# Gradient loads moved to the ScalarE queue and copies of P moved to GpSimd, in a fused window-attention forward and backward kernel

## Chip, cores, metric

One core of one Trainium2 chip. The metric is the device time of one execution in microseconds. All times are medians over the runs of one kernel. Runs are marked fast or slow (slow: over 1.5% above the fastest run of the same kernel). A ratio is the mean time of one kernel's fast runs over the mean of the other's fast runs of the same rounds, so it is not quite the ratio of the medians quoted beside it. Engines: PE is TensorE (matmuls), PEld its weight loads, DVE is VectorE, ACT is ScalarE, POOL is GpSimd, SP is SyncE. A "q" behind the name (SPq, ACTq) means the engine's sequencer, which issues DMAs. A DMA has landed when the semaphore (a counter that engines wait on) that tells of its end is full; its landing time is counted from its issue.

## The reference

Attention in windows of 8x8 tokens on a 256x256 picture with 384 channels, and its gradients. There is one head, and each window attends within itself.

```python
def _fwd_reference(x, wqkv, wo):            # x (1,256,256,384), cut to what matters
    xw = ...                                # 1024 windows of 64 tokens
    q, k, v = split(xw @ wqkv)
    p = softmax(q @ k.T * C ** -0.5)        # 64x64 per window
    return ((p @ v) @ wo).reshape(...)

def reference(x, wqkv, wo, grad_out):
    out, vjp = jax.vjp(_f, x, wqkv, wo)
    return (out, *vjp(grad_out))            # out, dx, dwqkv, dwo, all bfloat16
```

## The kernel before

The kernel works on 128 "quads" of four tiles, a tile being two windows (128 tokens on the 128 partitions). It is software-pipelined: in step i it takes quad i+1 through the projections (`A`), quad i through scores, softmax (whose first instruction on DVE takes the row maximum, `mx`) and half of its attention (`B`), quad i-1 through the other half (`C`), and quad i-2 through dx (`D`). The tile `xq` holds x, `dq` the incoming gradient. Four transposes a quad are done by DMA, all issued from SyncE: `dT` and `xT` (dq and xq with channels on the partitions), `tok` (`yz`, the output of the projections, turned to tokens) and `UT` (`Uq`, that is dS times x, turned for dx).

```python
def load(st):
    ...
    for t in range(QUAD):
        nc.sync.dma_start(out=xq[:, t, :], in_=dram_tile(x, bp, t0 + t))
        nc.gpsimd.dma_start(out=dq[:, t, :], in_=dram_tile(grad_out, bp, t0 + t))

# soft(), step 3, part 1: P into its places of the block tile ps
    for w, h in ((0, LO), (1, HI)):
        nc.scalar.copy(out=ps[h, :, w, :], in_=st["Pb"][h, :, :])

def step(d, c, b, a):          # "[...]" marks cuts
    B(scores) [... softmax of b on DVE/ACT between PE's values and projections ...]
    filler(1)                                   # PE: 12 matmuls of a weight gradient
    pw = C_(attend, (2, 3))                     # ACT copies osb, DVE copies Uq
    C_(to_channels, "Uq", "UT")                 # DMA transpose from SyncE
    C_(attend_end, (2, 3), pw)                  # ACT and DVE copy Wq
    D_(dx_tokens, (0, 1))
    turn_end(b, turn(b))                        # PE: pt; DVE: PS
    D_(dx, (0, 1))                              # PE: UT @ AT_sb; ACT copies dsb
    filler(1)
    pw = B(attend, (0, 1)) [...]
    D_(dx_tokens, (2, 3)); D_(dx, (2, 3))

for i in range(-1, n + 2):                      # LEAD = 3
    d, c, b, a = get(i - 2), get(i - 1), get(i), get(i + 1)
    to_channels(get(i + 2), "dq", "dT")         # SyncE: dT, xT, four xq, tok, then UT
    to_channels(get(i + 2), "xq", "xT")
    load(get(i + LEAD))
    to_tokens(c)
    step(d, c, b, a)
    [...]
```

All PSUM tiles come from one ring of eight. From `attend(2,3)` to `dx_tokens(0,1)` eight tiles are taken, so the next one, `pt` of `turn`, can only start when the first `osb` copy on ACT has freed its tile.

Of the kernel before, what the change touches and what calls it, by code (L numbers as in the profile page):

```python
# [17 lines left out]
QUAD = 4  # L18
# [4 lines left out]
def kernel(  # L23
# [12 lines left out]
    nc = tc.nc  # L36
# [7 lines left out]
    LEAD = 3  # L44
# [56 lines left out]
    def dram_tile(ap, bp, t):  # L101
        return ap[0, 2 * WIN * bp:2 * WIN * (bp + 1), WIN * t:WIN * (t + 1), :]
# [3 lines left out]
    def load(st):  # L106
        bp, t0 = st["at"]
        st["xq"] = xq = grp.tile([P, QUAD, C], BF16, tag="xq", name="xq", bufs=2 * GQ + 4)
        st["dq"] = dq = qp.tile([P, QUAD, C], BF16, tag="dq", name="dq", bufs=6)
        for t in range(QUAD):  # L110
            nc.sync.dma_start(out=xq[:, t, :], in_=dram_tile(x, bp, t0 + t))
            nc.gpsimd.dma_start(out=dq[:, t, :], in_=dram_tile(grad_out, bp, t0 + t))  # L112

    def to_channels(st, src, name):
        st[name] = dst = qp.tile([P, QUAD, CK, P], BF16, tag=name, name=name, bufs=3 if name == "xT" else 2)
        nc.sync.dma_start_transpose(out=dst[:].rearrange("p t m k -> p (t m) k"),
                                    in_=st[src][:].rearrange("p t c -> p (t c)"))
# [18 lines left out]
    def to_tokens(st):  # L136
        st["tok"] = tok = qp.tile([P, CK, QUAD, 2, P], BF16, tag="tok", name="tok")
        nc.sync.dma_start_transpose(out=tok[:].rearrange("p m t b k -> p (m t b) k"),
                                    in_=st["yz"][:].rearrange("p m t s k -> p (m t s k)"))
# [12 lines left out]
    def over_k(ap, n=P):  # L152
        return ap.unsqueeze(2).broadcast_to([n, QUAD, WT])

    def soft(st, step, part=0):
        sd = st["sd"]
        if step == 0:
            st["mx"] = mx = sm.tile([P, QUAD], F32, tag="mx", name="mx")
            for w, h in ((0, HI), (1, LO)):
                nc.vector.tensor_reduce(out=mx[h, :], in_=sd[h, :, w, :], axis=AX.X, op=ALU.max)  # L160
        elif step == 1:
            mx = st["mx"]
            st["sh"] = sh = sm.tile([P, QUAD, WT], F32, tag="sh", name="sh")
            for w, h, o in ((0, HI, LO), (1, LO, HI)):
                nc.vector.tensor_tensor(out=sh[o, :, :], in0=sd[h, :, w, :], in1=over_k(mx[h, :], WT),
                                        op=ALU.subtract)
        elif step == 2:
            st["ex"] = ex = sm.tile([P, QUAD, WT], F32, tag="ex", name="ex")
            nc.scalar.activation(out=ex[:], in_=st["sh"][:], func=ACT.Exp)  # L169
        elif step == 3 and part == 0:  # L170
            ex = st["ex"]
            rs = sm.tile([P, QUAD], F32, tag="rs", name="rs")
            nc.vector.tensor_reduce(out=rs[:], in_=ex[:], axis=AX.X, op=ALU.add)  # L173
            ri = sm.tile([P, QUAD], F32, tag="ri", name="ri")
            nc.vector.reciprocal(out=ri[:], in_=rs[:])
            st["Pb"] = Pb = qp.tile([P, QUAD, WT], BF16, tag="Pb", name="Pb")
            nc.vector.tensor_tensor(out=Pb[:], in0=ex[:], in1=over_k(ri[:]), op=ALU.mult)  # L177
        elif step == 3:
            st["ps"] = ps = qp.tile([P, QUAD, 2, WT], BF16, tag="ps", name="ps", bufs=3)
            for w, h in ((0, LO), (1, HI)):  # L180
                nc.scalar.copy(out=ps[h, :, w, :], in_=st["Pb"][h, :, :])
        elif step == 4:
            st["pr"] = pr = sm.tile([P, QUAD, WT], F32, tag="pr", name="pr")
            for w, h in ((0, LO), (1, HI)):
                nc.vector.tensor_tensor(out=pr[h, :, :], in0=sd[h, :, w, :], in1=st["Pb"][h, :, :], op=ALU.mult)  # L185
            st["D"] = D = sm.tile([P, QUAD], F32, tag="D", name="D")
            nc.vector.tensor_reduce(out=D[:], in_=pr[:], axis=AX.X, op=ALU.add)
        else:
            pd = sm.tile([P, QUAD, WT], F32, tag="pd", name="pd")
            nc.vector.tensor_tensor(out=pd[:], in0=st["Pb"][:], in1=over_k(st["D"][:]), op=ALU.mult)  # L190
            ps = st["ps"]
            for w, h, o in ((0, LO, HI), (1, HI, LO)):
                nc.vector.tensor_tensor(out=ps[o, :, w, :], in0=st["pr"][h, :, :], in1=pd[h, :, :], op=ALU.subtract)

    def turn(st):
        pt = ring.tile([P, QUAD, 2, WT], F32, tag="r", name="pt")
        for t in range(QUAD):
            both = st["ps"][:, t, :, :].rearrange("p w k -> p (w k)")
            for h in (LO, HI) if t < 2 else (slice(0, P),):
                nc.tensor.matmul(pt[h, t, :, :].rearrange("p s k -> p (s k)"), lhsT=both[:, h], rhs=ident[:],  # L200
                                 start=True, stop=True)
        return pt

    def turn_end(st, pt):
        st["PS"] = dst = qp.tile([P, QUAD, 2, WT], BF16, tag="PS", name="PS")
        nc.vector.tensor_copy(out=dst[:], in_=pt[:])
# [68 lines left out]
    def gf_group(sts):  # L275
        n = len(sts) * QUAD
        for f, rn in enumerate(("Uq", "Wq")):
            for ma in range(CK):
                pw = ring.tile([P, C], F32, tag="r", name="pg")
                for i in range(n):  # L280
                    st, t = sts[i // QUAD], i % QUAD
                    product(pw[:], st["xq"][:, t, ma * P:(ma + 1) * P], st[rn][:, t, :], i == 0, i == n - 1)
                nc.vector.tensor_tensor(out=GF_acc[:, f, ma, :], in0=pw[:], in1=GF_acc[:, f, ma, :], op=ALU.add)  # L283
                yield

    def filler(n):
        while n and fill:
            try:
                next(fill[0])
                n -= 1  # L290
            except StopIteration:
                fill.pop(0)

    def step(d, c, b, a):
        def on(st):
            return (lambda f, *r: f(st, *r)) if st is not None else (lambda f, *r: None)
        D_, C_, B, A = on(d), on(c), on(b), on(a)
        B(scores)
        B(soft, 0)
        B(soft, 1)  # L300
        B(values, 0)
        B(values, 1)
        B(values, 2)
        B(soft, 2)
        B(values, 3)
        B(soft, 3, 0)
        A(project, 0, 0)
        A(project, 0, 1)
        B(soft, 3, 1)
        A(project, 0, 2)  # L310
        B(soft, 4)
        A(project, 1, 0)
        B(soft, 5)
        A(project, 1, 1)
        A(project, 1, 2)
        filler(1)
        pw = C_(attend, (2, 3))
        C_(to_channels, "Uq", "UT")
        C_(attend_end, (2, 3), pw)
        D_(dx_tokens, (0, 1))  # L320
        if b is not None:
            turn_end(b, turn(b))
        D_(dx, (0, 1))
        filler(1)
        pw = B(attend, (0, 1))
        B(attend_end, (0, 1), pw)
        D_(dx_tokens, (2, 3))
        D_(dx, (2, 3))

    quads = [(bp, t0) for bp in range(NBP) for t0 in range(0, NT, QUAD)]  # L330
    sts = [{"at": q} for q in quads]
    n = len(sts)
    get = lambda i: sts[i] if 0 <= i < n else None
    with tc.manual_schedule(engines=MANUAL):
        for i in range(min(LEAD - 1, n)):
            load(sts[i])
        to_channels(sts[0], "dq", "dT")
        to_channels(sts[0], "xq", "xT")
        held = []
        for i in range(-1, n + 2):  # L340
            d, c, b, a = get(i - 2), get(i - 1), get(i), get(i + 1)
            if i + 2 > 0 and get(i + 2) is not None:
                to_channels(get(i + 2), "dq", "dT")
                to_channels(get(i + 2), "xq", "xT")
            if get(i + LEAD) is not None:
                load(get(i + LEAD))
            if c is not None:
                to_tokens(c)
            step(d, c, b, a)
            if c is not None:  # L350
                held.append(c)
            if held and (len(held) == GQ or i == n):
                fill.append(gf_group(held))
                held = []
            if 0 <= i - 2:
                sts[i - 2] = None
        filler(1 << 30)
# [62 lines left out]
```

## Time and profile before

| | before |
|---|---|
| time, median of 3 | 2122.46 us |
| a quad (span / 128, with the ends) | about 16.6 us |
| PE busy, idle | 1979 us, 142 us |
| SyncE's issues a quad, idle between them | 15.5 us, 0.8 us |

The page of the kernel before. The first line has the busy time of each engine, the next two what the packets of a DMA queue took as a share of 16 DMA engines' time (q1 is SyncE's queue, q0 GpSimd's), the last two the chain of work that ended last, by engine and by line.

```profile
PE 1979.2 (93%) x16510; PEld 1075.3 (51%) x16510; DVE 1268.9 (60%) x2851; ACT 1474.6 (70%) x3213; POOL 1124.8 (53%) x2054
...
q1 hardware_dynamic: 1074384, 304.15, 84.4%
q0 software_dynamic: 98304, 151.39, 26.9%
...
PE 55%; DMA 29%; DVE 7%; ACT 7%; issue 1%; POOL 0%; SPq 0%; ACTq 0%; POOLq 0%
DMA UT<-Uq 26%; PE pg L120 16%; PE pd L120 14%; PE pj L120 7%; PE pv L120 6%; ACT uq L219 5%; PE sd L147 4%; PE pd L262 4%; PE pu L237 3%; DMA tok<-yz 3%; DVE pr L185 2%; DVE rs L173 2%; ACT ex L169 2%; DVE Pb L177 2%; PE pw L237 1%
```

The two queues' packets add up to over 100%, because packets of different queues overlap on an engine. So the DMA engines are close to full. The timeline of SyncE (start, duration, what was issued) shows the queue that feeds them:

```profile
981.44 2.60 SPq L116 DMA_TRANSPOSE UT<-Uq  x1
984.26 3.20 SPq L116 DMA_TRANSPOSE dT<-dq  x1
987.64 2.82 SPq L116 DMA_TRANSPOSE xT<-xq  x1
990.52 2.54 SPq L111 DMA_DIRECT2D xq<-in_x_dram  x4
993.16 4.53 SPq L138 DMA_TRANSPOSE tok<-yz  x1
997.79 3.20 SPq L116 DMA_TRANSPOSE UT<-Uq  x1
```

There is no gap worth the name: 997.79 - 981.44 is one quad, and SyncE issues all through it. Since it runs late, PE waits for what it delivers. From the waits of the kernel before (who waited for whom: us in total, times, longest):

```profile
ACT osb L244 <- issue: 231.1, 152, 1.8
...
PE pd L262 <- DMA tok<-yz: 66.4, 57, 3.6
...
PE pd L120 <- DMA UT<-Uq: 53.0, 82, 2.9
```

ACT idles before `osb` copies with nothing to wait for (the first line), and PE's idle time is mostly for `UT` and `tok`. A piece of the timeline with ACT and PE at the first of these places; the bracket is idle time before, with what ended it:

```profile
1005.04 0.86 ACT L244 CAST osb<-po 128x384 bf16<-128x384 f32 x2 [1.50 <-issue]
...
1005.21 0.52 PE L262 MATMUL pd<-tok,ps 128*64 128x384 bf16 x4
1005.57 0.52 PE L200 MATMUL pt<-ident,ps 128*64 128x128 bf16 x6
```

`pt` follows at once, because `osb` was copied in time.

### The profile page before, as it was taken

The page shows a single profiled execution, that of the slowest core. Times are in us where ns is not written, and L with a number is a line of the kernel's source. Part 1 is how long each engine was busy: PE and PEld are TensorE (multiplying, and loading weights), DVE is VectorE, ACT ScalarE, POOL GpSimd, SP SyncE. Part 2 cuts the span into 40 slices and gives each one's busy share as a digit, 9 for nine tenths or more (in the row PEclk, how much of TensorE's full clock was granted, in tenths as well). Part 3 has the DMA queues.
Part 4 walks back from the last instruction along what each step waited for, and adds up shares of the span by engine and source line. Part 5 has one row for each costly group of instructions (what it writes and reads, how often), then busy time and mean ns, then how long its engine had stood idle before and what let it go on. Part 6 is the DMA issues. An engine that isn't in the chain of part 4 may idle for free.

```text
span 2121.0 us, 46307 instructions
## 1 busy us (share of the span) xinstructions
PE 1979.2 (93%) x16510; PEld 1075.3 (51%) x16510; DVE 1268.9 (60%) x2851; ACT 1474.6 (70%) x3213; POOL 1124.8 (53%) x2054
## 2 busy tenths in 40 slices
PE   7899999999999999989999998999999999999998
PEld 4455555555555555544555454555555454455554
DVE  6566566656656655655556555665566655556664
ACT  6677677767767767766667666776677766767773
POOL 4555555555555555555555455555555555555543
PEclk9999999999999999999999999999999999999999
DMA  9999999999999999999999999999999999999995
GB/s 208 219 221 224 214 224 229 225 217 211 224 230 217 226 218 219 219 217 206 219 217 216 205 226 213 212 215 216 228 217 220 221 216 216 212 219 225 225 222 124
DMA packets 1173319, 458.79 MB, mean 216 GB/s; under 512 B 1056864, under 2 KB 1147744, under 8 KB 1173088
## 3 DMA queue, kind: packets, MB, share of 16 engines
q1 hardware_dynamic: 1074384, 304.15, 84.4%
q0 software_dynamic: 98304, 151.39, 26.9%
q8 instruction: 129, 2.11, 0.5%
q14 instruction: 102, 0.84, 0.1%
q10 hardware_dynamic: 400, 0.29, 0.0%
HBM read 101.84 MB, written 101.84 MB: 96 GB/s over the span
## 4 chain that ended last, share of the span: by engine, by line
PE 55%; DMA 29%; DVE 7%; ACT 7%; issue 1%; POOL 0%; SPq 0%; ACTq 0%; POOLq 0%
DMA UT<-Uq 26%; PE pg L120 16%; PE pd L120 14%; PE pj L120 7%; PE pv L120 6%; ACT uq L219 5%; PE sd L147 4%; PE pd L262 4%; PE pu L237 3%; DMA tok<-yz 3%; DVE pr L185 2%; DVE rs L173 2%; ACT ex L169 2%; DVE Pb L177 2%; PE pw L237 1%
## 5 line engine op out<-in xcount | busy, mean ns | idle before, releaser
L226 POOL DMA_DIRECT2D out_dram<-osb x1024 | 580.5, 574 | 671.1 <-ACT osb L244 641.3
L244 ACT CAST osb<-po 128x384 bf16<-128x384 f32 x512 | 220.7, 483 | 411.7 <-issue 231.1
L283 DVE TENSOR_TENSOR GF_acc<-pg,GF_acc 128x384 f32<-128x384 f32 x258 | 143.9, 558 | 548.0 <-PE pg L120 548.0
L120 PEld LDWEIGHTS <-xq 128*128 128x128 bf16 x3072 | 304.9, 99 | 221.0 <-issue 14.3
L112 POOL DMA_DIRECT2D dq<-in_grad_out_dram x512 | 270.4, 534 | 190.2 <-DMA out_dram<-osb 172.2
L120 PE MATMUL pd<-AT_sb,UT 128*128 128x384 bf16 x1536 | 305.5, 337 | 53.5 <-DMA UT<-Uq 53.0
L228 POOL DMA_DIRECT2D out_dram<-dsb x512 | 275.9, 543 | 115.3 <-ACT dsb L270 101.3
L270 ACT CAST dsb<-pd 128x384 bf16<-128x384 f32 x512 | 229.6, 481 | 148.1 <-issue 111.6
L120 PE MATMUL pg<-Wq,xq 128*128 128x384 bf16 x1536 | 277.4, 332 | 0.0
L120 PE MATMUL pg<-Uq,xq 128*128 128x384 bf16 x1536 | 273.5, 329 | 0.0
L120 PE MATMUL pv<-B_sb,xT 128*128 128x384 bf16 x1536 | 271.4, 327 | 0.0
L120 PE MATMUL pj<-xT,A_sb 128*128 128x512 bf16 x1152 | 269.5, 379 | 0.7 <-DMA xT<-xq 0.7
L120 PE MATMUL pj<-dT,BT_sb 128*128 128x512 bf16 x1152 | 269.5, 379 | 0.0
L219 ACT CAST uq<-pv 128x384 bf16<-128x384 f32 x512 | 242.9, 475 | 36.3 <-PE pv L120 34.2
L245 DVE CAST Uq<-pu 128x384 bf16<-128x384 f32 x512 | 259.3, 548 | 3.1 <-PE pu L237 3.1
L256 ACT CAST Wq<-pw 64x384 bf16<-64x384 f32 x512 | 242.9, 474 | 9.2
L132 ACT CAST yz<-pj 128x512 bf16<-128x512 f32 x384 | 225.4, 587 | 4.3 <-PE pj L120 0.2
L120 PEld LDWEIGHTS <-UT 128*128 128x128 bf16 x1536 | 133.2, 99 | 171.1 <-DMA UT<-Uq 69.9
L134 ACT CAST yz<-pj 128x512 bf16<-128x512 f32 x384 | 201.3, 603 | 1.1 <-PE pj L120 1.0
L262 PE MATMUL pd<-tok,ps 128*64 128x384 bf16 x1024 | 133.4, 340 | 71.1 <-DMA tok<-yz 66.4
L120 PEld LDWEIGHTS <-xT 128*128 128x128 bf16 x1536 | 141.8, 98 | 83.4 <-issue 0.8
L120 PEld LDWEIGHTS <-A_sb 128*128 128x128 bf16 x1152 | 112.7, 98 | 136.9 <-DMA xT<-xq 1.2
(61 smaller groups left out, 2020.8 us busy)
## 6 DMA issues: line engine op xcount, KB each, us to landing
xq<-in_x_dram SPq DMA_DIRECT2D x512, 96.0 KB, 3.9
dq<-in_grad_out_dram POOLq DMA_DIRECT2D x512, 96.0 KB, 5.8
out_dram<-osb POOLq DMA_DIRECT2D x1024, 48.0 KB, 4.3
out_dram<-dsb POOLq DMA_DIRECT2D x512, 96.0 KB, 4.8
dT<-dq SPq DMA_TRANSPOSE x128, 5.5
xT<-xq SPq DMA_TRANSPOSE x128, 5.3
tok<-yz SPq DMA_TRANSPOSE x128, 10.0
UT<-Uq SPq DMA_TRANSPOSE x128, 6.1
```

What stands on the lines that cost most here:

```text
L112: nc.gpsimd.dma_start(out=dq[:, t, :], in_=dram_tile(grad_out, bp, t0 + t))
L120: nc.tensor.matmul(out, lhsT=lhsT, rhs=rhs, start=start, stop=stop)
L132: nc.scalar.copy(out=yz[:, mo, :, 0:4:3, :], in_=pj[:])
L134: nc.scalar.copy(out=yz[:, mo, :, 1:3, :], in_=pj[:])
L219: nc.scalar.copy(out=st["uq"][:, t, :], in_=pj[:])
L226: nc.gpsimd.dma_start(out=to[WIN * w:WIN * (w + 1)], in_=src[h, :])
L228: nc.gpsimd.dma_start(out=to, in_=src[:])
L244: nc.scalar.copy(out=osb[:], in_=po[:])
L245: nc.vector.tensor_copy(out=st["Uq"][:, t, :], in_=pu[:])
L256: nc.scalar.copy(out=st["Wq"][h, pair[1], :], in_=pw[1][o, :])
L262: nc.tensor.matmul(pd[o, :], lhsT=st["ps"][:, t, w, :], rhs=st["tok"][:, :, t, w, :], start=True, stop=False)
L270: nc.scalar.copy(out=dsb[:], in_=pd[:])
```

## The change

Its intent: GpSimd's queue carries all stores and the gradient loads; take the gradient loads off it, to a hardware-driven queue, and issue them from ACT exactly where ACT idles. ACT gets room for that by giving the two small copies of P to GpSimd.

```diff
-            nc.gpsimd.dma_start(out=dq[:, t, :], in_=dram_tile(grad_out, bp, t0 + t))
+    def load_grad(st, tiles):
+        bp, t0 = st["at"]
+        for t in tiles:
+            nc.scalar.dma_start(out=st["dq"][:, t, :], in_=dram_tile(grad_out, bp, t0 + t))
 [...]
-                nc.scalar.copy(out=ps[h, :, w, :], in_=st["Pb"][h, :, :])
+                nc.gpsimd.tensor_copy(out=ps[h, :, w, :], in_=st["Pb"][h, :, :])
 [... in step(), ahead is quad i + 3 ...]
         filler(1)
+        if ahead is not None:
+            load_grad(ahead, (0, 1))
         pw = C_(attend, (2, 3))
 [...]
         D_(dx, (0, 1))
+        if ahead is not None:
+            load_grad(ahead, (2, 3))
         filler(1)
         pw = B(attend, (0, 1))
```

More of the change, by code (lines that the diff above doesn't have):

```diff
@@ L292, in filler, with step @@
                 fill.pop(0)
-    def step(d, c, b, a):
+    def step(d, c, b, a, ahead):
         def on(st):
@@ L336 @@
             load(sts[i])
+            load_grad(sts[i], range(QUAD))
         to_channels(sts[0], "dq", "dT")
@@ L348 @@
                 to_tokens(c)
-            step(d, c, b, a)
+            step(d, c, b, a, get(i + LEAD))
             if c is not None:
```

## The prediction

> **What bounds the kernel now.** The 128 quads cost 16.4 us each, and two limits share that time. (1) DMA: packet times add up to 84.4% (SyncE's queue) plus 26.9% (GpSimd's) of 16 engines; the DMA row stands at 9 in all slices but the last. The timeline of SyncE is back to back: per quad about 2.4 (UT), 2.7 (dT), 1.9 (xT), 3.1 (four xq), 5.5 us (tok), 15.7 of 16.4, although the shortest of each seen add up to 10.5[...]. The queue runs so late that UT is issued about 11 us after Uq is written, and the chain of waits gives 26% of the span to UT<-Uq. (2) PE: busy 93%, idle some 140 us, 120 of them waiting for UT and tok. So about 6% is the most that relief of the DMA can give.
>
> **What the change moves, per quad.** GpSimd loses four gradient issues (0.53 us each) and gains two copies of 64x256; ACT loses those copies (0.81 us) and gains four issues. xq's issues on SyncE take 0.54 us at least, 0.61 in the median, so I estimate 2.2 to 2.8 us on ACT, net +1.4 to +2, on an engine 70% busy. They stand where ACT idles about 1.5 us, before the osb copies. GpSimd is no limit; its copies (estimate: under 1 us together) end long before turn reads ps. DVE and PE keep their work. The freed ACT time buys nothing: PE hardly waits for ACT there.
>
> **DMA.** The bytes stay. The Trainium skill (DMA: Bandwidth & Descriptors, "Issuing engines are not separate DMA queues") says that all DMAs run on the same 16 engines and interleave; the trace agrees: SyncE's packets in flight fall from 19 to 1 while GpSimd's fill the engines. From the packet records, 6144 B of gradient per engine cost about 350 ns as 4608+1536 B packets of GpSimd's queue; as eight 768 B packets, as xq has them, 288 at best, 350 on average. Gain: 0 to 0.25 us per quad, 0 to 1.5%.
>
> **New coupling.** SyncE and ACT share eight DMA semaphores in rotation; now twelve DMAs per quad take turns. In the built program the second gradient load of a step waits for dT of the same step to have landed, the third and fourth for xq's first two. dT is issued about 6.6 us after the step's first maximum and lands 5.5 us later, at 12, while ACT reaches this load at about 7. ACT would stand over 4 us; osb holds a PSUM buffer that turn needs, so PE would stand too. That delay lets SyncE catch up by 3 to 4 us, until ACT's stall is about the 1.2 us that PE loses today. I expect this balance: the wait for UT largely vanishes, a wait for ACT (osb) appears, the pace stays the DMA's. Fluctuating landings (dT up to 8.8 us) then cost 1 to 2%.
>
> **Prediction: 2135 us**, 80% range 2065 to 2250. Faster by over 2%: 0.20; within 2%: 0.45; slower by over 2%: 0.35.
>
> **To be seen if right:** waits for UT under half; ACT idle before gradient issues for DMA dT or xq, PE before pt for ACT osb; SyncE's issues still back to back; dT issued 3 to 4 us earlier in the step; GpSimd busy below 950 us, DVE unchanged.
>
> **What would make it wrong.** If smaller gradient packets let transposes through, SyncE's sum per quad falls below 15 us and PE nears its own limit: 2030 to 2070. If ACT's issues take over 1 us each behind SyncE's transposes, or the shared semaphores hold ACT without SyncE catching up: 2200 to 2300.

## The result

| | before | after |
|---|---|---|
| median (4 runs each) | 2121.81 us | 2245.00 us |
| ratio of fast runs, 95% interval | | 1.056 (1.050 to 1.063) |
| PE busy, idle in the profiled run | 1979 us, 142 us | 2030 us, 221 us |
| mean granted TensorE clock | 0.987 | 0.962 |

The page of the kernel after, the same lines; q10 is ACT's queue:

```profile
PE 2029.8 (90%) x16510; PEld 1099.1 (49%) x16510; DVE 1278.3 (57%) x2851; ACT 1410.2 (63%) x2957; POOL 960.5 (43%) x1798
...
q1 hardware_dynamic: 1074384, 304.15, 83.0%
q0 software_dynamic: 73728, 101.02, 17.7%
q10 hardware_dynamic: 74128, 50.66, 9.3%
...
PE 69%; DMA 24%; ACTq 3%; ACT 3%; issue 1%; DVE 1%; SPq 0%; DVEq 0%
DMA dT<-dq 22%; PE pj L124 16%; PE pg L124 15%; PE pd L124 13%; PE pv L124 11%; PE sd L151 4%; PE pu L241 3%; PE pt L204 3%; PE pd L266 3%; ACTq L116 2%; ACT osb L248 2%; PE pw L241 1%; DMA dq<-in_grad_out_dram 1%; DMA UT<-Uq 0%; DMA xT<-xq 0%
```

The transpose on the chain is no longer `UT` but `dT`. The waits of the kernel after answer to those above; the second block is the longest of SyncE's own waits for a DMA, which before had only small ones (1.8 us for gradients):

```profile
ACT osb L248 <- DMA dT<-dq: 263.7, 58, 6.5
...
PE pt L204 <- ACT osb L248: 196.3, 100, 3.9
...
PE pd L266 <- DMA tok<-yz: 2.1, 1, 2.1
...
PE pd L124 <- DMA UT<-Uq: 0.7, 1, 0.7
```

```profile
SPq L120 <- DMA dq<-in_grad_out_dram: 255.7, 162, 4.3
```

PE's waits for `UT` and `tok` are gone (119 to 3 us); in their place PE waits 196 us before `pt` for ACT, and ACT stands for a DMA. The timeline at the place shown before:

```profile
1005.07 3.73 ACTq L116 DMA_DIRECT2D dq<-in_grad_out_dram  x2
...
1007.52 0.52 PE L266 MATMUL pd<-tok,ps 128*64 128x384 bf16 x4
...
1008.99 0.86 ACT L248 CAST osb<-po 128x384 bf16<-128x384 f32 x2 [3.33 <-DMA dq<-in_grad_out_dram]
1009.52 0.52 PE L204 MATMUL pt<-ident,ps 128*64 128x128 bf16 x6 [1.48 <-ACT osb L248]
...
1011.12 0.55 ACTq L116 DMA_DIRECT2D dq<-in_grad_out_dram  x1
...
1011.71 1.03 ACTq L116 DMA_DIRECT2D dq<-in_grad_out_dram  x1
```

The first two gradient loads hold ACT 3.73 us, though one takes 0.55 us to issue: the second waits. And SyncE, from its timeline, now has a hole in each quad, before `dT`:

```profile
1000.32 2.05 SPq L120 DMA_TRANSPOSE UT<-Uq  x1
1002.80 2.83 SPq L120 DMA_TRANSPOSE dT<-dq  x1
1005.68 1.53 SPq L120 DMA_TRANSPOSE xT<-xq  x1
1007.26 3.11 SPq L111 DMA_DIRECT2D xq<-in_x_dram  x4
1010.47 5.08 SPq L142 DMA_TRANSPOSE tok<-yz  x1
1015.65 2.87 SPq L120 DMA_TRANSPOSE UT<-Uq  x1
1019.93 2.63 SPq L120 DMA_TRANSPOSE dT<-dq  x1
```

From 1018.52 to 1019.93 SyncE issues nothing.

To see who waits for whom in the mean, I took from the traces the times of issue and landing in each step, counted from the step's first `mx` on DVE, and formed medians over 115 quads (of the experiments too; each is explained below). The columns of SyncE are sums of its issues and of the gaps between them per quad, with the gap before `dT` in brackets.

| kernel | dT issued / landed | 2nd gradient load issued | last gradient load issued / landed | SyncE issuing, idle (before dT) | mean quad |
|---|---|---|---|---|---|
| before | 6.6 / 12.0 | 2.1 | 5.2 / 9.9 | 15.5, 0.8 (0.2) | 16.27 |
| after | 4.1 / 9.43 | 9.45 | 12.95 / 21.06 | 14.6, 2.7 (2.2) | 17.28 |
| loads_only | 4.1 / 9.1 | 9.1 | 12.5 / 20.7 | 14.7, 2.4 (2.0) | 17.11 |
| touch | 2.1 / 9.2 | 4.2 | 5.3 / 10.8 | 16.0, 0.8 (0.2) | 16.81 |
| lead | 2.5 / 9.0 | 6.4 | 13.4 / 21.1 | 15.8, 0.7 (0.2) | 16.50 |
| lead_touch | 2.9 / 9.4 | 6.4 | 12.8 / 20.9 | 16.3, 0.7 (0.2) | 16.98 |
| late_pool | 6.3 / 11.5 | 5.0 | 13.5 / 17.6 | 15.4, 0.9 (0.3) | 16.30 |
| one_three | 5.3 / 10.8 | 12.4 | 14.3 / 23.0 | 14.6, 2.6 (2.1) | 17.23 |
| sp_loads | 8.7 / 14.6 | 16.0 | 19.0 / 22.3 | 16.2, 0.9 (0.2) | 17.14 |

In the kernel after, the second gradient load is issued 0.02 us after `dT` of the same step has landed. In the built program it waits for exactly that: the DMAs of SyncE and ACT take turns on eight semaphores, each waits until the one that had its semaphore before has landed, and `dT` is eight DMAs back. This wait is tight: it is under 0.2 us in 97% of the 115 steps. And `dT` of the next step, which reads what the last gradient load brings, is issued 0.07 to 0.19 us after that load has landed (tenth to ninetieth percentile). So the row closes a loop: dT to its landing 5.3, from there through ACT's copies, and the matmuls of PE that these wait for, to the last gradient load 3.5, to its landing 8.1, to the next dT the rest of the quad of 17.3 us. That these parts add up to a quad proves nothing, because the next `dT` comes one quad after this one in any kernel; what speaks for the loop is that neither of the two waits in it has slack.

That is theory L. Its rivals when the experiments began: I, ACT's four issues cost ACT too much time; D, gradients in 768 B packets cost the DMA engines more than in the 4608 and 1536 B packets of GpSimd's queue; C, the copies on GpSimd come late. Two more, S and T, came up on the way: S, the stall of ACT is the whole cost and needs no loop; T, late gradients alone are.

### The profile page after: what moved, and what is told of

Same layout as the page of the kernel before. It is cut to its first block, busy times and chain, and to the rows that moved or that the text cites. A ratio compares the mean times of both kernels' runs of the same rounds, so it can differ in the third digit from the quotient of the medians.

```text
span 2251.2 us, 45972 instructions
## 1 busy us (share of the span) xinstructions
PE 2029.8 (90%) x16510; PEld 1099.1 (49%) x16510; DVE 1278.3 (57%) x2851; ACT 1410.2 (63%) x2957; POOL 960.5 (43%) x1798
## 4 chain that ended last, share of the span: by engine, by line
PE 69%; DMA 24%; ACTq 3%; ACT 3%; issue 1%; DVE 1%; SPq 0%; DVEq 0%
DMA dT<-dq 22%; PE pj L124 16%; PE pg L124 15%; PE pd L124 13%; PE pv L124 11%; PE sd L151 4%; PE pu L241 3%; PE pt L204 3%; PE pd L266 3%; ACTq L116 2%; ACT osb L248 2%; PE pw L241 1%; DMA dq<-in_grad_out_dram 1%; DMA UT<-Uq 0%; DMA xT<-xq 0%
## 5 line engine op out<-in xcount | busy, mean ns | idle before, releaser
L124 PEld LDWEIGHTS <-xq 128*128 128x128 bf16 x3072 | 315.2, 103 | 242.5 <-issue 48.6
L124 PE MATMUL pd<-AT_sb,UT 128*128 128x384 bf16 x1536 | 325.4, 353 | 0.7 <-DMA UT<-Uq 0.7
L124 PE MATMUL pg<-Wq,xq 128*128 128x384 bf16 x1536 | 295.4, 346 | 0.0
L124 PE MATMUL pg<-Uq,xq 128*128 128x384 bf16 x1536 | 281.4, 335 | 0.0
L204 PE MATMUL pt<-ident,ps 128*64 128x128 bf16 (+1 forms) x768 | 72.3, 236 | 200.5 <-ACT osb L248 196.3
L274 ACT CAST dsb<-pd 128x384 bf16<-128x384 f32 x512 | 224.3, 481 | 40.6 <-PE pd L124 19.4
L138 ACT CAST yz<-pj 128x512 bf16<-128x512 f32 x384 | 224.8, 588 | 23.0
L136 ACT CAST yz<-pj 128x512 bf16<-128x512 f32 x384 | 224.6, 587 | 15.5 <-PE pj L124 0.2
L124 PEld LDWEIGHTS <-UT 128*128 128x128 bf16 x1536 | 143.2, 104 | 109.9 <-issue 49.8
L210 DVE CAST PS<-pt 128x512 bf16<-128x512 f32 x128 | 88.2, 689 | 167.6 <-PE pt L204 167.4
L164 DVE TENSOR_REDUCE mx<-sd 64x4 f32<-64x256 f32 x256 | 108.1, 422 | 125.8 <-PE sd L151 121.8
```

The source lines that it names most:

```text
L124: nc.tensor.matmul(out, lhsT=lhsT, rhs=rhs, start=start, stop=stop)
L136: nc.scalar.copy(out=yz[:, mo, :, 0:4:3, :], in_=pj[:])
L138: nc.scalar.copy(out=yz[:, mo, :, 1:3, :], in_=pj[:])
L204: nc.tensor.matmul(pt[h, t, :, :].rearrange("p s k -> p (s k)"), lhsT=both[:, h], rhs=ident[:], start=True, stop=True)
L274: nc.scalar.copy(out=dsb[:], in_=pd[:])
```

## The experiments

Each was timed in three rounds (pool_lead in five) against the kernel before on the same chip, up to four kernels sharing the runs of before; all outputs were correct.

### copies_only

```diff
 # the kernel before, with
-                nc.scalar.copy(out=ps[h, :, w, :], in_=st["Pb"][h, :, :])
+                nc.gpsimd.tensor_copy(out=ps[h, :, w, :], in_=st["Pb"][h, :, :])
```

> Only the copies of P go to GpSimd; gradient loads stay on GpSimd's queue as before. Theory L (a loop of waits through the gradient loads on ACT and the shared DMA semaphores) expects no loss: 2100 to 2135 us, ACT busy about 105 us less than before. Rival C (the copies on GpSimd, in order behind stores, delay ps and hence turn, or hold up the stores) expects most of the loss here: 2190 us or more.

Measured: 2128.24 us beside 2132.00 of before in these rounds, ratio 0.999 (0.997 to 1.002). ACT's busy time fell from 1474.6 to 1415.7 us (59 us, where 105 were expected), and nothing came of it. Rival C falls for the copies by themselves, and the freed ACT time is worth nothing.

### loads_only

```diff
 # the kernel after, with
-                nc.gpsimd.tensor_copy(out=ps[h, :, w, :], in_=st["Pb"][h, :, :])
+                nc.scalar.copy(out=ps[h, :, w, :], in_=st["Pb"][h, :, :])
```

> Only the gradient loads go to ACT's queue; ACT keeps the copies of P. Theory L expects nearly all of the loss: 2220 to 2270 us, with the second gradient load of a step issued as dT of that step lands, and dT issued as the last gradient load lands. Rival C expects about 2120 to 2150.

Measured: 2229.69 us, ratio 1.046 (1.042 to 1.050). The loss is in the gradient loads. As expected, the second load goes out when `dT` lands, and the two waits are as tight again: under 0.2 us from dT's landing to the second load in 99% of the steps, and 0.07 to 0.19 us from the last load's landing to the next dT. One thing is left over: beside these loads the copies on GpSimd cost about 1% more (2253 us for the same program with both, the next run), though alone they cost nothing. No run explains that.

### rotation

```diff
 # the kernel after: dT, xT, xq and tok are emitted after the first two gradient loads
+        sync_block()          # behind load_grad(ahead, (0, 1)), no longer ahead of step()
```

> The changed kernel with every engine's instructions in the same order, but the program emits SyncE's block (dT, xT, xq, tok) after the first two gradient loads. So the rotation of the eight DMA semaphores falls otherwise: the first two gradient loads of a step wait for xq loads of the step before, long landed, and the last two for dT and xT of the same step. Theory L: the stall of ACT before the first osb (some 370 us in total for DMA) mostly goes, the loop is cut at that place, 2090 to 2160 us. Rival I (ACT's four issues cost it about 2.9 us a quad) and rival D (gradients as 768 B packets on a third queue cost the DMA engines more) expect no change: 2220 to 2260, since issues and packets are the same.

Measured: 2253.36 us, ratio 1.058 (1.054 to 1.062). This experiment failed as an experiment. I had believed that the order in the source decides which DMA gets which semaphore; the built program has the same instructions in the same order with the same semaphores as the kernel after. So it is a repeat of the kernel after, and says only that its loss repeats.

### lead

```diff
 # the kernel after, gradients one quad further ahead (the six buffers of dq suffice)
-        for i in range(min(LEAD - 1, n)): load(sts[i]); load_grad(sts[i], range(QUAD))
+        for i in range(min(LEAD - 1, n)): load(sts[i])
+        for i in range(min(LEAD, n)): grad_tile(sts[i]); load_grad(sts[i], range(QUAD))
-            step(d, c, b, a, get(i + LEAD))
+            grad_tile(get(i + LEAD + 1)); step(d, c, b, a, get(i + LEAD + 1))
```

> The changed kernel with gradients loaded one quad further ahead (four steps before their use by turn of SyncE's dT becomes due instead of three; the six buffers suffice). The rotation is as in the changed kernel, so the second load still waits for dT of the same step, but dT no longer waits for a gradient that has just been issued. Theory L: the loop is cut at the other place; SyncE's wait for gradients (256 us) goes, dT is issued earlier in the step, ACT's stall shrinks: 2090 to 2170 us. Rivals I and D expect no change, 2220 to 2260; if only the shared semaphore costs and not the loop, about 2200 to 2250 too.

Measured: 2149.64 us, ratio 1.008 (1.005 to 1.011). Nearly all of the loss is gone, with the same issues on ACT, the same packets, the same queues and the same copies on GpSimd. So rivals I and D by themselves can account for about 1% at most. The run does not cut the loop at one place alone, though. The built program shows that the semaphores fell otherwise here: the first two gradient loads wait for gradient loads of the step before, no longer for `dT`. SyncE's wait for gradients shrinks from 255.7 us to 6.0 (the first block, from SyncE's own waits), and the longest wait of PE before `pt` in the loop is for DVE (the second block), no longer 196.3 us for ACT:

```profile
SPq L122 <- DMA dq<-in_grad_out_dram: 6.0, 4, 2.4
```

```profile
PE pt L206 <- DVE ps L199: 1.7, 4, 0.8
...
PE sd L153 <- ACT osb L250: 132.5, 89, 3.4
```

ACT is not free of waits here, as the last line shows: the third load starts 0.02 us after the second x load of the same step has landed, so ACT stands there for 1.6 us a step in the mean, and PE waits before `sd` instead of `pt`.

To tell the stall of ACT from the loop, the next three were needed.

### touch

```diff
 # the kernel before, nothing of the change
         filler(1)
+        if new is not None:                     # new is quad i + 2
+            nc.scalar.copy(out=touched[0:1, :], in_=new["dT"][0:1, 0, 0, 0:1])
         pw = C_(attend, (2, 3))
```

> The kernel before, and nothing of the change, but ACT copies one element of this step's dT just before the first osb of the step, so that ACT stands there until dT has landed, as in the changed kernel. Gradients are still loaded early from GpSimd's queue, so no loop closes. Theory L: SyncE runs ahead until the stall is small, 2115 to 2165 us, dT issued 3 to 5 us earlier in the step than before (6.6 us). Rival S (the stall of ACT for dT is the whole cost, with or without a loop): 2190 to 2260.

Measured: 2188.05 us, ratio 1.031 (1.027 to 1.034). The waits of this kernel:

```profile
ACT touched L320 <- DMA dT<-dq: 312.9, 111, 5.5
...
PE pt L200 <- ACT osb L244: 158.0, 84, 4.0
```

One copy of one element (193 ns) that makes ACT wait for `dT` costs over half of what the change costs. SyncE does run ahead, `dT` is issued 4.5 us earlier in the step, as theory L and the prediction had it; but it lands only 2.8 us earlier (9.2 instead of 12.0), because there it takes 7.1 us instead of 5.4 to land. So ACT still stands 2.8 us (312.9 / 111) when it stands. There is no loop through the gradients here. 2188 is above L's 2165 and just below S's 2190: L's expectation missed, and S explains more than half of the loss.

### lead_touch

```diff
 # the kernel lead, with the one-element copy of dT behind the first gradient loads
             load_grad(ahead, (0, 1))
+        nc.scalar.copy(out=touched[0:1, :], in_=new["dT"][0:1, 0, 0, 0:1])
```

> The kernel that loads gradients one quad further ahead from ACT's queue (it took 2150 us, and there the rotation happened to fall so that no gradient load waits for dT of its step), with the one-element copy on ACT that waits for this step's dT. So the stall is back, but dT waits for no fresh gradient. Theory L: 2140 to 2185 us. Rival S: 2215 or more.

Measured: 2218.32 us, ratio 1.045 (1.041 to 1.048). The stall alone takes `lead` from 1.008 to 1.045, with SyncE's queue back to back (idle 0.7 us, 0.2 before dT). (Its copy starts 0.08 us after the landing of dT in most steps.) This is S's number, not L's.

### late_pool

```diff
 # the kernel after, with
-            nc.scalar.dma_start(out=st["dq"][:, t, :], in_=dram_tile(grad_out, bp, t0 + t))
+            nc.gpsimd.dma_start(out=st["dq"][:, t, :], in_=dram_tile(grad_out, bp, t0 + t))
```

> The changed kernel with its late places of the gradient loads, but issued from GpSimd's queue: dT must wait for fresh gradients, while nothing waits for dT on ACT and the eight semaphores of SyncE are its own. Theory L: no loop, 2115 to 2170 us. Rival T (late gradients alone hold SyncE and cost the time): 2200 us or more.

Measured: 2114.45 us, ratio 0.995 (0.991 to 0.999). The gradients are loaded as late in the step as in the kernel after, but land in 4.0 us instead of 8.1 (17.6 - 13.5), nothing on ACT waits for `dT`, and SyncE hardly waits for them. The landing differs in more than the queue: `tok` is issued after these loads here (14.6 us into the step) and before them in the kernel after (11.2). The first block below is from SyncE's own waits, the second from the other engines':

```profile
SPq L120 <- DMA dq<-in_grad_out_dram: 20.7, 15, 3.3
```

```profile
PE pd L124 <- DMA UT<-Uq: 96.6, 90, 2.3
```

So rival T falls: lateness alone costs nothing. The whole loss sits in the one word `scalar` in place of `gpsimd`. PE's wait for `UT` is back, as in the kernel before. This is the only version here that beats both kernels, by half a per cent (less than the 2% from which a run is called faster).

### one_three

```diff
 # the kernel after, with
-            load_grad(ahead, (0, 1))
+            load_grad(ahead, (0,))
 [...]
-            load_grad(ahead, (2, 3))
+            load_grad(ahead, (1, 2, 3))
```

> The changed kernel with only the first gradient load at the first place and the other three at the second. In the built program the first then waits for a gradient load of the step before, the other three for xT and two xq of the same step, about when ACT gets there anyway. So the stall before the first osb goes, while dT still waits for gradients that are loaded late in the step before. Theory S (the stall before the first osb is the main cost; it cost 3.1% by itself): 2120 to 2170 us. Theory L (the closed loop is the main cost): 2190 to 2240, with SyncE idle about 2 us a quad before dT as in the changed kernel.

Measured: 2245.07 us, ratio 1.058 (1.053 to 1.062). Its waits, in the second block SyncE's own:

```profile
PE sd L151 <- ACT osb L248: 152.7, 88, 4.3
...
DVE PS L210 <- PE pt L204: 20.0, 20, 3.3
```

```profile
SPq L120 <- DMA dq<-in_grad_out_dram: 243.2, 165, 4.5
```

The stall before the first `osb` did go: DVE's wait for `pt`, 167.4 us in the kernel after, is 20.0. But nothing was won. SyncE idles 2.1 us before `dT` as in the kernel after, and the loop now runs over `xT`, which SyncE issues behind `dT`, and the three loads at the second place: the second load starts 0.02 us after `xT` has landed, the next `dT` 0.07 us after the last load has (medians; the landing of the last load is known in 57 of the 115 steps). ACT stands at this place instead, so that PE waits before `sd`. This is L's number. The stall at the first place is not needed for the loss as long as the loop is closed. The stall at the second place does not explain the loss either: `lead` has one of about the same size (PE before `sd` 132.5 us, here 152.7) and no loop, and it loses 0.8% where this kernel loses 5.8%. Of all runs, this pair comes closest to a test of the loop alone.

### sp_loads

```diff
 # the kernel before, with
-            nc.gpsimd.dma_start(out=dq[:, t, :], in_=dram_tile(grad_out, bp, t0 + t))
+            nc.sync.dma_start(out=dq[:, t, :], in_=dram_tile(grad_out, bp, t0 + t))
```

> The kernel before with the gradient loads on SyncE's queue, each next to its xq: the same 768 B packets as in the changed kernel, no load on ACT and none of GpSimd. Theory L: 2110 to 2190 us (above before only as far as SyncE's issue rate binds, up to 2.4 us more issuing a quad). Rival D (768 B packets in place of the 4608 and 1536 B ones cost the DMA engines the lost time): 2220 us or more, with a mean of 256 B packets above 27 ns.

Measured: 2243.09 us, ratio 1.057 (1.053 to 1.061), far outside what theory L allowed. It is not D either: the 256 B packets of the transposes took 23.5 ns on average, less than before (25.9), and fewer packets were in flight. What binds, by its trace, is SyncE's own time. From its timeline:

```profile
1009.36 0.60 SPq L111 DMA_DIRECT2D xq<-in_x_dram  x1
1010.00 1.85 SPq L112 DMA_DIRECT2D dq<-in_grad_out_dram  x1
```

A gradient load takes SyncE 0.60 us in the median (the second line shows a longer one), the four new ones 2.8 us a quad, and SyncE has no idle time to put them in: 16.2 us of issues a quad. That is another reason than the changed kernel's, where SyncE issued 14.6 us and idled.

### xq_pool, xq_pool_late and pool_lead: a better kernel?

If SyncE's queue sets the pace, taking the x loads (3.1 us a quad) off it should help. Three tries:

```diff
 # xq_pool: the kernel before; xq_pool_late: late_pool; each with
-            nc.sync.dma_start(out=xq[:, t, :], in_=dram_tile(x, bp, t0 + t))
+            nc.gpsimd.dma_start(out=xq[:, t, :], in_=dram_tile(x, bp, t0 + t))
 # pool_lead: the kernel lead, x loads and gradient loads on gpsimd, copies of P on scalar
```

> The opposite of the change, for a better kernel: before, with the x loads moved from SyncE's queue to GpSimd's as well. SyncE then issues transposes only; its issues of xq took 3.1 us of 16.4 a quad, at a rate that leaves the DMA engines partly empty. If SyncE's queue sets the pace: 2040 to 2100 us. If the DMA engines as such do: 2105 to 2140. If GpSimd's queue, in order behind waiting stores, delays the loads: slower, 2140 or more.

> The same move of the x loads to GpSimd's queue, on the kernel with the late gradient loads on GpSimd's queue and the copies of P there (2114 us). If SyncE's queue sets the pace: 2035 to 2095 us. If the DMA engines do: 2100 to 2130. If GpSimd's queue (then busy some 70%) becomes the limit: 2140 or more.

> For a better kernel: x loads and gradient loads both on GpSimd's queue, gradients one quad further ahead and spread over two places of the step, copies of P on ACT as before. In the kernel where only the x loads were moved to that queue beside late gradients, SyncE stood 2.8 us a quad before dT for gradients, and PE waited for the copies on GpSimd; both reasons are taken away here. If SyncE's queue sets the pace: 2040 to 2095 us, with SyncE issuing 13 to 14 us a quad and less than 0.5 us idle before dT. If the DMA engines set it: 2100 to 2135, with SyncE's issues stretched to 15 us or more. If GpSimd's queue is the limit, its issues waiting for the landing of earlier ones: 2140 or more.

Measured: 2408.14 us, ratio 1.131 (1.123 to 1.139); 2170.10 us, ratio 1.024 (1.019 to 1.029); 2179.23 us, ratio 1.026 (1.021 to 1.031), with one of its six runs slow, which the ratio leaves out. All three are worse than before. SyncE did get room, 13.3 and 13.7 us of issues a quad in the last two, but stood still for 3.2 and 3.1 us a quad, mostly (2.7 and 2.3) for loads that GpSimd's queue, in order behind stores, delivered late. The first block is SyncE's longest wait for a DMA in xq_pool_late, the second the same of pool_lead, the third ACT's longest wait in pool_lead:

```profile
SPq L120 <- DMA dq<-in_grad_out_dram: 349.6, 130, 7.8
```

```profile
SPq L122 <- DMA xq<-in_x_dram: 289.5, 92, 7.0
```

```profile
ACT osb L250 <- DMA out_dram<-osb: 436.1, 165, 6.7
```

In pool_lead, ACT also stood 436 us for stores that had not left. So by these waits GpSimd's queue becomes the limit, as the third case of the expectations had it, and whether SyncE's queue or the DMA engines set the pace of the kernel before stays open.

## Why the prediction was right or wrong

- **What bounds the kernel before: held.** SyncE's queue is back to back and PE waits for `UT`. Moving ACT's or GpSimd's work alone changed nothing (copies_only 0.999, late_pool 0.995). Which of the two, SyncE's queue or the DMA engines behind it, sets the pace is not shown.
- **"The freed ACT time buys nothing": shown** by copies_only.
- **The new coupling: shown as the cause.** The second load waited for `dT`, ACT stood, `osb` held PSUM, PE waited before `pt`, the waits for `UT` and `tok` vanished. `lead`, where no gradient load waits for a transpose any more (its third still waits for an x load), loses 0.8%; `late_pool`, where nothing on ACT waits for SyncE, loses nothing.
- **"Until ACT's stall is about the 1.2 us that PE loses today": wrong.** This is the step that failed first. It took for granted that a `dT` issued earlier lands that much earlier. `touch` shows 4.5 us earlier at the issue but 2.8 at the landing, and 2.8 us of stall left; the stall alone then costs 3.1%, not "1 to 2%". In the kernel after, `dT` is issued and lands only 2.5 us earlier, held back by the loop below, and ACT stands 3.1 us in the median between its first and its second load, not 1.2.
- **"The pace stays the DMA's", "SyncE's issues still back to back": wrong.** In the kernel after SyncE idles 2.2 us a quad before `dT`, for gradients that land 8.1 us after their issue. The prediction listed that dT stalls ACT's gradient loads, but not that `dT` itself waits for what those loads bring. With that the waits close into a loop of 17.3 us. Before, the last gradient load landed in 4.8 us (9.92 - 5.15, medians of the step's times); with that in place of 8.1 I estimate the loop at 14.0 us, less than a quad, so that it would not have bound. So the failed term is the gradients' landing, 8.1 us in place of 4.8, in a sum that the prediction did not write down. Why the last loads take so long to land was not tested, but the five traces with gradients on ACT's queue looked at for this (`after`, `loads_only`, `lead`, `lead_touch`, `one_three`) share a pattern: gradient loads issued before SyncE begins to issue `tok` land in 2.7 to 4.4 us, those issued while it issues `tok` (11.2 to 16.5 us in the step of the kernel after) in 6.9 to 8.3 (medians by place). So the landing time of a load depended on where in the step it was issued, and the last two stood in a bad place.
- **Stall and loop do not add up, and they overlap.** Stall without loop: 1.031 and 1.045. Loop without the stall at the first place: 1.058. Both: 1.056. A stall at the second place without the loop: 1.008 (`lead`). Why SyncE's back-to-back issues take 16.0 and 16.3 us a quad in `touch` and `lead_touch`, instead of 15.5, is open; the bytes are the same.
- **PE pays twice, and the prediction left that out.** PE's idle time grew by 79 us (142 to 221), but its busy time grew too, by 51 us for the same 16510 matmuls. Within the span the clock records show 16 stretches at half clock, 56 us together, before, and 42 with 171 us after; half of the added 115 us is 57 us, close to the 51. The Trainium skill (TensorE: Matmul & The Clock Gate, "What's actually happening") says that an idle window of about 3.4 us sets the clock to half until PE has been busy; the trace agrees in the length of the stretches, 3.413 us or multiples of it, but for the last one, which the end of the run cuts.
- **Size.** "2135 us" was 110 us short. That the time still lies in the range, at its upper end, is more luck than foresight: the balance behind 2135 did not come about, and the cost that did was in no sum of the prediction. It lies beside the case "2200 to 2300", whose condition, "the shared semaphores hold ACT without SyncE catching up", comes near. SyncE caught up by 2.5 us of the 3 to 4, and GpSimd's busy time fell to 960 instead of under 950 us.
- **DMA cost: no gain.** "0 to 1.5%" of gain cannot be seen in any kernel with 768 B gradient packets; the best of them, `lead`, is 0.8% slower than before.

## What to carry to other kernels

Moving a DMA to another engine's queue does not only move its issue time: the instruction waits in that engine's order, for its buffer and for its semaphore, and if the semaphores are shared out in turn, for DMAs of another queue. Look in the built program for what each moved DMA waits for, follow the chain until it comes back to itself, and add it up with the landing times that the new place will have; if the sum reaches the time of an iteration, the loop is the new pace. An engine whose copies free PSUM is a costly place for such a wait (3.1% in `touch`), so fill its idle slots only with instructions whose waits you have followed.

## What the Trainium skill lacked or had wrong

- DMA: Bandwidth & Descriptors, "Why a DMA increments its semaphore by 16 and not by 1", asks for one semaphore per in-flight slot. It does not say what it costs when there are fewer semaphores than DMAs in flight and two engines share them: here ACT stood for SyncE's transpose, and a stall of that kind alone cost 3.1% (`touch`).
- The same page, "Issuing engines are not separate DMA queues", says that issuing from several engines only saves the sequencer's time, which is usually small beside the DMA itself. That compares one issue with its DMA, and it was small here too (0.60 us of SyncE in the median for a 96 KB load that lands in 3.5 us); what counted was the sum in one queue: SyncE issued for 15.5 us of a 16.3 us quad, and four more loads a quad on it cost 5.7% (`sp_loads`).
- The same page calls the hardware-driven queues generally faster ("Issuing engine by pattern"). Here that depended on the place in the step: from ACT's queue the first two gradient loads of a step landed in 3.6 and 2.7 us and the last two in 7.0 and 8.3 (`after`); from GpSimd's they landed in 4.6 and 5.0, and in 3.8 and 4.1 (`late_pool`). Neither queue was faster throughout.
- TensorE: Matmul & The Clock Gate, "What's actually happening", names an idle window of about 3.4 us as the condition for half clock. In the kernel after, the longest idle time in the 6.8 us before such a stretch was 2.4 us in the median (2.2 before), and PE was busy for about a third of the last 3.4 us (0.32, before 0.34), with PE's ends modelled; so the window need not be idle throughout.
